# Fused attention and softplus FFN on one core: the reciprocals' store on another queue, another order in the last round, and transposes nobody reads

## The chip, the cores and the metric

One core of one Trainium2 chip. The metric is the device time of one execution in microseconds (us), median of several runs. The engines are TensorE (PE; its weight loads are listed as PEld), VectorE (DVE), ScalarE (ACT), GpSimd (POOL) and SyncE (SP), which here only issues DMAs. TensorE's clock has two levels, 2.4 and 1.2 GHz; the profile prints the granted share, 1.00 and 0.50.

## The reference, cut to what matters

```python
# q, k, v: (4, 8, 576, 64) float32; w_in: (512, 2048), w_out: (2048, 512), given as float64
scores = scale * np.matmul(q, k.transpose(0, 1, 3, 2)) + bias      # bias: a small MLP of log distances
attn = np.exp(scores - np.max(scores, axis=-1, keepdims=True))
attn = attn / (np.sum(attn, axis=-1, keepdims=True) + 1e-09)
x = np.matmul(attn, v).transpose(0, 2, 1, 3).reshape(2304, 512)
h = x @ w_in
out = (np.maximum(h, 0.0) + np.log1p(np.exp(-np.abs(h)))) @ w_out
```

## The kernel before

The work has three stages. The first (to about 65 us) writes the bias table to DRAM (`e_d`). The second is the attention: 16 units n = 0 to 15, each a pair of heads of one batch item. The third is the FFN over blocks of tokens (512 at a time, one of 256), 16 slices of the hidden dimension each, in float32 split in two float32r parts.

One unit of attention has nine score tiles t. `u_s` (L314) computes a tile on TensorE into PSUM (L338; tokens S, Z), adds the bias and takes the minimum on VectorE (L356; A, ZA), and takes the exponential and its row sums on ScalarE (L374; X, ZX). `u_t` (L409) transposes blocks of the exponentials on TensorE (`turn`, L402; T) and copies them from PSUM to `pt` (L310 on ScalarE, L312 on VectorE; V). The letter behind the slash of a T names the PSUM tile that it writes (0 and 1: the two `s` tiles, 2: `t`, o: the tile of the attention output `o`, beside its accumulators); behind a V it names the engine of the copy (a: ScalarE, d: VectorE). `u_pv` (L442) multiplies by v into `o` (L461; P0 to P4; P3 and P4 belong to the unit of the round before). The reciprocals of the row sums (`inv`, L494; I) are transposed (`u_r`, R), copied to a tile `r` of 9 x 128 on ScalarE (L515; C), stored to `r_d` in DRAM (L516), and 24 tokens later read back from there, spread over 64 partitions, as `rb` by three DMAs (L522). `u_x` (L472; O, one round later) multiplies `o` by `rb` on VectorE (L481) into `x`, which four DMAs store to `x_d` (L487 to L490), the input of the FFN. `queue(n)` (L502) picks the queue of the store and of the reads: ScalarE's for units 0 and 1, SyncE's for the others.

The order on every engine is written out by hand: one string of tokens for each round (`ROUND0`, L52, for unit 0, `ROUND` for units 2 to 13, `ROUND15`, L73, for the last), read from left to right by `emit` (L569). The instructions of a token go to the end of their engines' queues in that order, and each engine works through its own in order. Between them stand the loads of later units on SyncE's queue (L98), and the preparation of FFN weights: float64 weights are read (L660), reduced to float32 (L635 to L652; B) and stored (`w_d`, L673).

Round 15 also starts the FFN. Its f tokens name entries of `FIRST` (L82): f2 is `w_fin` (L714) for the first slice of `w_in`, an ScalarE copy (L719) that waits for the load of `w_d` (L691) and a GpSimd subtraction (L721); f3, f0, f7, f9 prepare the four parts of the first block's `x` (L737 on ScalarE, L738 on VectorE), f4 loads the last of them; f11 and f12 are the first two steps, whose matmuls (`emit_h`, L742, L748) write one of four PSUM tiles `h`. PSUM tiles of the attention's scores are given up before round 15, and the `h` tiles lie there.

`es_m` keeps the order as emitted; waits between engines are inserted by the framework where tiles are shared.

Of the kernel before, what the change touches and what calls it, by code (L numbers as in the profile page):

```python
# [9 lines left out]
F32 = mybir.dt.float32  # L10
# [10 lines left out]
B, H, S, D = 4, 8, 576, 64  # L21
# [7 lines left out]
SH = S // 2  # L29
# [20 lines left out]
"""  # L50

ROUND0 = """  # L52
A6 A2 Z7 T10/1 A7 Z3 T20/0 V20/a T30/o A0 T00/2 ZA7 V00/d V30/a V10/a A1 A5 Z8 X7 X2 ZX7 ZA3 X5
X6 ZA8 A3 ZX3 ZX8 Z4 ZA4 ZL1 ZL3 ZX4 A8 T22/2 T40/1 T32/o ZL4 V32/d T02/0 V22/a V02/a T01/o X0
T11/2 V40/d T21/1 V11/a ZL2 V01/d V21/d L2 T12/0 P0 X8 L0 X1 I V12/d T41/1 A4 P1 X4 T31/0 R/2
V41/a C P2 V31/d L3 X3 L4 L1
"""
# [13 lines left out]
"""  # L71

ROUND15 = """  # L73
P3 I T00/2 P4 V00/a T02/2 V02/d f2 T32/2 V32/a T10/2 O R/o V10/a C T01/o V01/a T11/o T12/2 V11/a
V12/a T22/o V22/a f4 P0 T21/2 f3 V21/a f0 P1 T20/2 V20/a f7 T30/2 V30/a T40/2 f8 f1 V40/a f9 f11
B0 T41/2 P2 B1 f5 f10 V41/d f6 T31/2 B2 B3 f12 V31/a B4
"""
ROUND16 = """
P3 P4 O
# [41 lines left out]
def tile_log_bias_attention__then__softplus_ffn(  # L121
# [13 lines left out]
    nc = tc.nc  # L135
# [5 lines left out]
    r_d = dram.tile([16, 9, 128], F32, name="r_d")  # L141
# [9 lines left out]
    ident = const.tile([128, 128], F32, name="ident")  # L151
# [108 lines left out]
    N = 16  # L260
# [120 lines left out]
    def tail(n, i):  # L381

        assert all(("e", n, t) in done for t in TAILS[i])
        done.add(("l", n, i))
        tl = pp.tile([128, 2, 64], F32, tag="tl", name="tl", bufs=9)
        if i < 4:
            src = pairs.pop((n, i))[:, :, 512:S]
        else:
            src = prob[n, 4][:, 512:S].rearrange("p (o c) -> p o c", o=1)
            src = src.to_broadcast([128, 2, 64])  # L390
        nc.gpsimd.tensor_copy(tl, src)
        tails[n, i] = tl.rearrange("p a c -> p (a c)")

    s_use, s_held = [0], set()

    def turn(blocks, on=None):
        ps = ps_o if on == "o" else s_buf[int(on)]
        ps = ps[:, :, SH:SH + 64 * len(blocks)].rearrange("p a (i c) -> p a i c", c=64)
        for i, src in enumerate(blocks):
            for a in range(2):  # L400
                rows = slice(64 * a, 64 * a + 64)
                nc.tensor.transpose(  # L402
                    ps[:, a, i], src[rows], ident[rows, 64 * a:64 * a + 64], tile_position=(64 * a, 0)
                )
        return ps
# [88 lines left out]
    def inv(n):  # L494

        assert all(("e", n, t) in done for t in range(9))
        done.add(("i", n))
        s_ = ssum[n][:, 0:9]
        nc.vector.tensor_scalar(s_, s_, 1e-9, None, op0=ALU.add)
        nc.vector.reciprocal(s_, s_)  # L500

    def queue(n):  # L502
        return nc.scalar if n < 2 else nc.sync

    def u_r(n):

        st_ = {}

        def pe(on=None):
            assert ("i", n) in done  # L510
            st_["ps"] = turn([ssum[n]], on)

        def first():
            r = st.tile([9, 128], F32, tag="r", name="r")
            nc.scalar.activation(r.rearrange("p (a c) -> p a c", a=2), st_["ps"][0:9, :, 0], AF.Copy)  # L515
            queue(n).dma_start(out=r_d[n], in_=r)  # L516

        def second():
            t = op_.tile([128, S], F32, tag="rb", name="rb")
            flat = r_d[n].rearrange("a b -> (a b)").rearrange("(o c) -> o c", o=1)  # L520
            for hd, lo, hi, c0 in ((0, 0, S, 0), (1, 256, S, S), (1, 0, 256, S + 320)):
                queue(n).dma_start(  # L522
                    out=t[64 * hd:64 * hd + 64, lo:hi],
                    in_=flat[:, c0:c0 + hi - lo].to_broadcast([64, hi - lo]),
                )
            rb[n] = t

        return pe, first, second
# [40 lines left out]
    def emit(n, tok):  # L569

        tok, _, on = tok.partition("/")
        on = (on,) if on else ()
        kind, late_ = tok.rstrip("0123456789"), tok[len(tok.rstrip("0123456789")):]
        a = [int(c) for c in late_]

        def stage(key, make, i, *arg):
            if key not in units:
                units[key] = make(*key[1:])
            units[key][i](*arg)

        if kind in ("S", "A", "X"):
            if n + 1 < N:
                stage(("s", n + 1, *a), u_s, "SAX".index(kind))
        elif kind in ("Z", "ZA", "ZX"):
            stage(("s", n, *a), u_s, ("Z", "ZA", "ZX").index(kind))
        elif kind == "L":
            if n + 1 < N:
                tail(n + 1, *a)
        elif kind == "ZL":
            tail(n, *a)  # L590
        elif kind in ("T", "V"):
            stage(("t", n, *a), u_t, "TV".index(kind), *on)
        elif kind == "P":
            stage(("p", n - (a[0] >= PV_LATE), *a), u_pv, 0)
        elif kind == "I":
            inv(n)
        elif kind in ("R", "C"):
            stage(("r", n), u_r, "RC".index(kind), *on)
        elif kind == "O":
            if n:  # L600
                stage(("x", n - 1), u_x, 0)
                defer(8, lambda: stage(("x", n - 1), u_x, 1))
        elif kind == "B":
            if 1 <= n <= len(pre):
                stage(("b", n - 1), u_bits, *a)
                if a[0] == 4:
                    defer(8, lambda: stage(("b", n - 1), u_bits, 5))
        elif kind == "f":
            w, *arg = FIRST[int(late_)]
            FFN[w](*arg)  # L610
        else:
            assert False, tok
# [3 lines left out]
    def defer(k, f):  # L616
        waiting.append([k, f])
# [59 lines left out]
    fp = {}  # L677
# [63 lines left out]
    hs, gs, ys = {}, {}, {}  # L741
    def emit_h(bi, f):  # L742
        nb = blocks[bi][1]
        ps = fp["h"].tile([128, 512], F32, tag="h", name="h")
        i = 0
        for c in range(4):
            for a, x_ in ((0, 0), (0, 1), (1, 0)):
                nc.tensor.matmul(  # L748
                    ps[:, :nb],
                    lhsT=wi[f][:, a, 128 * c:128 * c + 128],  # L750
                    rhs=xs[bi, c][:, x_, :nb],
                    start=(i == 0),
                    stop=(i == 11),
                )
                i += 1
        hs[bi, f] = ps
# [105 lines left out]
    ps_t, ps_o = (ps_a.tile([128, 2, 512], F32, name=nm) for nm in ("t", "o"))  # L862
# [21 lines left out]
    def step(i):  # L884

        new = old = None
        if i < len(seq):
            bi, f = seq[i]
            emit_h(bi, f)
# [156 lines left out]
```

## Time and profile before

| | |
|---|---|
| median of 3 runs | 703.2 us (702.04, 703.2, 712.35) |
| the profiled execution: its own time | 707.46 us |
| its span, first to last instruction | 705.6 us |
| busy share of the span: PE, PEld, DVE, ACT, POOL | 94%, 67%, 71%, 73%, 6% |
| mean granted clock of TensorE | 0.971 |

Times in the rows are microseconds from the start of the span unless marked ns. A row of the timeline gives start, duration, engine, line, operation, out<-in, how many instructions were merged, and in brackets the idle time ahead of them with what ended it. Rows whose engine ends in q (SPq, ACTq) are instructions of a queue that issue DMAs; their duration is the issue, not the transfer. A PE that counts as busy need not run at its peak.

### The profile page before, as it was taken

How to read it: one execution, taken by the hardware profiler on the slowest of the kernel's cores; microseconds unless marked ns; L12 is line 12 of the kernel's file. 1: busy time of each engine (PE TensorE's matmuls, PEld its weight loads, DVE VectorE, ACT ScalarE, POOL GpSimd, SP SyncE). 2: the span in 40 equal slices, each digit the busy share in tenths (PEclk: the TensorE clock that was granted, in tenths of full speed). 3: DMA queues.
4: the chain of work that ended last, by engine and by line, in shares of the span. 5: the costliest groups of instructions: out<-in, count | busy, mean ns of one | idle time of the engine just before them, and what ended most of it. 6: DMA issues, size and time to landing. Idle time of an engine off the chain costs nothing.

```text
span 705.6 us, 13216 instructions
## 1 busy us (share of the span) xinstructions
PE 661.3 (94%) x4800; PEld 475.7 (67%) x4800; DVE 499.8 (71%) x1078; ACT 514.8 (73%) x1062; POOL 40.6 (6%) x106
## 2 busy tenths in 40 slices
PE   5697889998998999599999999999999999999997
PEld 2123446555655665368788888888888888888886
DVE  6996568976887889267888694778686554655564
ACT  6899568986887899477777675886676575665654
POOL 0000111121111111110000000000000000000000
PEclk9898799999999999799999999999999999999999
DMA  5885967677776653545132210521020320402220
GB/s 152 309 275 173 344 177 226 195 227 237 231 232 232 214 182 101 177 124 178 61 135 74 90 59 2 179 90 60 31 90 1 105 75 2 151 28 83 67 84 37
DMA packets 51041, 96.85 MB, mean 137 GB/s; under 512 B 7440, under 2 KB 19104, under 8 KB 50976
## 3 DMA queue, kind: packets, MB, share of 16 engines
q1 hardware_dynamic: 50460, 95.41, 41.3%
q8 instruction: 38, 0.62, 0.4%
q10 hardware_dynamic: 516, 0.60, 0.4%
q14 instruction: 27, 0.22, 0.1%
HBM read 67.98 MB, written 28.01 MB: 136 GB/s over the span
## 4 chain that ended last, share of the span: by engine, by line
PE 77%; DMA 11%; ACT 4%; DVE 3%; SPq 2%; issue 2%; ACTq 0%; DVEq 0%
PE h L748 27%; PE y L806 26%; PE o L461 8%; PE s L338 6%; PE acc L230 3%; PE s L402 3%; DMA r_d<-r 3%; DMA rb<-r_d 2%; DMA e_d<-e 2%; PE t L338 2%; PE t L402 2%; ACT e L251 1%; DMA b<-e_d 1%; PE o L402 1%; SPq L522 1%
## 5 line engine op out<-in xcount | busy, mean ns | idle before, releaser
L748 PE MATMUL h<-x,wi 128*128 128x512 f32 (+1 forms) x960 | 213.9, 372 | 0.1
L806 PE MATMUL y<-wo,g 128*128 128x512 f32 x864 | 209.9, 391 | 0.0
L748 PEld LDWEIGHTS h<-x,wi 128*128 128x128 f32 x960 | 170.4, 190 | 33.9 <-DVE wi L721 0.9
L806 PEld LDWEIGHTS y<-wo,g 128*128 128x128 f32 x864 | 161.3, 188 | 33.7 <-DVE g L780 0.2
L771 DVE SCALAR_TENSOR_TENSOR u<-u,e 128x512 f32<-128x512 f32 (+1 forms) x80 | 51.0, 637 | 102.2 <-ACT l L768 101.9
L374 ACT ACTIVATE p<-p,m 128x576 f32<-128x576 f32 x144 | 110.1, 767 | 8.8 <-DVE m L356 6.7
L764 ACT ACTIVATE e<-h 128x512 f32<-128x512 f32 (+1 forms) x80 | 44.2, 553 | 78.9 <-PE h L748 78.9
L461 PE MATMUL o<-pt,vn 128*64 128x256 f32 (+3 forms) x640 | 91.3, 430 | 0.6 <-ACT pt L310 0.6
L356 DVE CUSTOM_DVE_ANT_0 p<-s,b 128x576 f32<-128x576 f32 x92 | 68.5, 755 | 26.1 <-PE s L338 9.0
L338 PE MATMUL s<-kn,qn 64*128 64x288 f32 (+1 forms) x468 | 69.5, 436 | 0.2 <-ACT p L349 0.2
L778 ACT ACTIVATE g<-l 128x512 fp32r<-128x512 f32 (+1 forms) x80 | 46.8, 585 | 20.4 <-DVE l L775 10.7
L461 PEld LDWEIGHTS o<-pt,vn 128*64 128x64 f32 (+1 forms) x640 | 37.1, 140 | 28.5 <-issue 13.3
L780 DVE TENSOR_TENSOR g<-l,g 128x512 fp32r<-128x512 f32 (+1 forms) x80 | 50.4, 630 | 3.7 <-ACT g L778 3.7
L230 PE MATMUL acc<-m,coef 128*32 128x512 f32 (+17 forms) x352 | 37.7, 527 | 14.5 <-DVE m L217 7.2
L775 DVE TENSOR_TENSOR l<-l,u 128x512 f32<-128x512 f32 (+1 forms) x80 | 50.6, 633 | 0.0
L773 DVE SCALAR_TENSOR_TENSOR l<-h,l 128x512 f32<-128x512 f32 (+1 forms) x80 | 50.5, 631 | 0.0
L768 ACT ACTIVATE l<-u 128x512 f32<-128x512 f32 (+1 forms) x80 | 47.1, 589 | 2.9 <-DVE g L780 0.2
L765 ACT ACTIVATE e<-e 128x512 f32<-128x512 f32 (+1 forms) x80 | 47.2, 590 | 2.5
L767 ACT ACTIVATE u<-e 128x512 f32<-128x512 f32 (+1 forms) x80 | 47.2, 590 | 2.6
L402 PEld LDWEIGHTS s<-ident,p 64*128 64x128 f32 x546 | 26.8, 141 | 29.6 <-issue 8.2
L217 DVE TENSOR_SCALAR m<-lw,pb 128x576 f32<-128x576 f32 (+17 forms) x122 | 44.3, 445 | 0.4 <-PE acc L230 0.4
L338 PEld LDWEIGHTS s<-kn,qn 64*128 64x128 f32 (+1 forms) x468 | 31.0, 176 | 15.4 <-issue 8.4
(66 smaller groups left out, 685.3 us busy)
## 6 DMA issues: line engine op xcount, KB each, us to landing
e_d<-e SPq DMA_DIRECT2D x36, 295.5 KB, 4.0
qn<-in_q_dram SPq DMA_DIRECT2D x16, 576.0 KB, 5.4
b<-e_d SPq DMA_DIRECT2D x32, 288.0 KB, 4.0
r<-in_moe_w_in_dram SPq DMA_DIRECT2D x16, 512.0 KB, 5.1
r<-in_moe_w_out_dram SPq DMA_DIRECT2D x16, 512.0 KB, 3.1
xr<-x_d SPq DMA_DIRECT2D x28, 256.0 KB, 3.4
vn<-in_v_dram SPq DMA_DIRECT2D x16, 320.0 KB, 3.3
kn<-in_k_dram SPq DMA_DIRECT2D x16, 288.0 KB, 6.6
```

The costliest lines, as they stand in the source:

```text
L230: nc.tensor.matmul(acc[32 * g:32 * g + 32, lo:hi], lhsT=coef.rearrange("p o h -> p (o h)"), rhs=hid[s, g][:, lo:hi], start=True, stop=True ...
L338: nc.tensor.matmul(ps[at:at + w, half, :SH], lhsT=q_n[n][rows, hd, c0:c0 + w], rhs=k_n[n][rows, hd], start=True, stop=True, tile_position= ...
L356: nc.vector.tensor_tensor_reduce(prob[n, t].rearrange("p (a c) -> p a c", a=2), st_["ps"], bias[pr, t].rearrange("p (a c) -> p a c", a=2), ...
L374: nc.scalar.activation(p, p, AF.Exp, bias=st_["m"], scale=-1.0, accum_out=ssum[n][:, PLACE.index(t):PLACE.index(t) + 1],)
L402: nc.tensor.transpose(ps[:, a, i], src[rows], ident[rows, 64 * a:64 * a + 64], tile_position=(64 * a, 0))
L461: nc.tensor.matmul(o[up, half, 0:w], lhsT=v_n[n][rows, jb, hd], rhs=pt[n, jb][rows, c0:c0 + w], start=(jb == 0), stop=(jb == 4), tile_posi ...
L748: nc.tensor.matmul(ps[:, :nb], lhsT=wi[f][:, a, 128 * c:128 * c + 128], rhs=xs[bi, c][:, x_, :nb], start=(i == 0), stop=(i == 11),)
L771: nc.vector.scalar_tensor_tensor(u, u, -1.0, e, op0=ALU.add, op1=ALU.subtract)
L773: nc.vector.scalar_tensor_tensor(l, ps, 0.0, l, op0=ALU.max, op1=ALU.add)
L775: nc.vector.tensor_tensor(l, l, u, op=ALU.subtract)
L780: nc.vector.tensor_tensor(g[:, 1], l, g[:, 0], op=ALU.subtract)
L806: nc.tensor.matmul(y, lhsT=g[:, a, 128 * ts:128 * ts + 128], rhs=wo[f][:, w_], start=(first and i == 0), stop=(last and i == 2),)
```

## The change

Three things. (1) The store of the reciprocals, L516, is issued from ScalarE's queue in every unit; the reads back (L522) stay where they were. (2) A new token D*k* issues k transposes of the 128 x 128 identity by itself on TensorE; nothing reads what they write. In round 0 (D6 ahead of Z8, D14 ahead of T22) they write columns 288 to 415 of the first bank of the tile `o`, cells that only the transposes marked /o use; in round 15 (D4, D4, D6) they write one of the four `h` tiles, which the FFN's first step then takes over. (3) Round 15 gets another order: T32 and its copy go from behind V02 to behind V01, and its copy from ScalarE to VectorE; the copy V02 goes from VectorE to ScalarE, V01, V22 from ScalarE to VectorE, V41 from VectorE to ScalarE; f2 goes from ahead of T32 to behind T12, ahead of V11; I goes behind T00; B0 goes ahead of f11.

```diff
@@ -50,8 +50,8 @@
 """
 
 ROUND0 = """
-A6 A2 Z7 T10/1 A7 Z3 T20/0 V20/a T30/o A0 T00/2 ZA7 V00/d V30/a V10/a A1 A5 Z8 X7 X2 ZX7 ZA3 X5
-X6 ZA8 A3 ZX3 ZX8 Z4 ZA4 ZL1 ZL3 ZX4 A8 T22/2 T40/1 T32/o ZL4 V32/d T02/0 V22/a V02/a T01/o X0
+A6 A2 Z7 T10/1 A7 Z3 T20/0 V20/a T30/o A0 T00/2 ZA7 V00/d V30/a V10/a A1 A5 D6 Z8 X7 X2 ZX7 ZA3 X5
+X6 ZA8 A3 ZX3 ZX8 Z4 ZA4 ZL1 ZL3 ZX4 A8 D14 T22/2 T40/1 T32/o ZL4 V32/d T02/0 V22/a V02/a T01/o X0
 T11/2 V40/d T21/1 V11/a ZL2 V01/d V21/d L2 T12/0 P0 X8 L0 X1 I V12/d T41/1 A4 P1 X4 T31/0 R/2
 V41/a C P2 V31/d L3 X3 L4 L1
 """
@@ -71,9 +71,9 @@
 """
 
 ROUND15 = """
-P3 I T00/2 P4 V00/a T02/2 V02/d f2 T32/2 V32/a T10/2 O R/o V10/a C T01/o V01/a T11/o T12/2 V11/a
-V12/a T22/o V22/a f4 P0 T21/2 f3 V21/a f0 P1 T20/2 V20/a f7 T30/2 V30/a T40/2 f8 f1 V40/a f9 f11
-B0 T41/2 P2 B1 f5 f10 V41/d f6 T31/2 B2 B3 f12 V31/a B4
+P3 T00/2 D4 I P4 V00/a T02/2 D4 V02/a T10/2 D6 O R/o V10/a C T01/o V01/d T32/2 V32/d T11/o T12/2 f2 V11/a
+V12/a T22/o V22/d f4 P0 T21/2 f3 V21/a f0 P1 T20/2 V20/a f7 T30/2 V30/a T40/2 f8 f1 V40/a f9 B0
+f11 T41/2 P2 B1 f5 f10 V41/a f6 T31/2 B2 B3 f12 V31/a B4
 """
 ROUND16 = """
 P3 P4 O
@@ -392,6 +392,7 @@
         tails[n, i] = tl.rearrange("p a c -> p (a c)")
 
     s_use, s_held = [0], set()
+    spare = {}
 
     def turn(blocks, on=None):
         ps = ps_o if on == "o" else s_buf[int(on)]
@@ -513,7 +514,7 @@
         def first():
             r = st.tile([9, 128], F32, tag="r", name="r")
             nc.scalar.activation(r.rearrange("p (a c) -> p a c", a=2), st_["ps"][0:9, :, 0], AF.Copy)
-            queue(n).dma_start(out=r_d[n], in_=r)
+            nc.scalar.dma_start(out=r_d[n], in_=r)
 
         def second():
             t = op_.tile([128, S], F32, tag="rb", name="rb")
@@ -605,6 +606,12 @@
                 stage(("b", n - 1), u_bits, *a)
                 if a[0] == 4:
                     defer(8, lambda: stage(("b", n - 1), u_bits, 5))
+        elif kind == "D":
+            if n == N - 1 and "h" not in spare:
+                spare["h"] = fp["h"].tile([128, 512], F32, tag="h", name="h")
+            to = spare["h"][:, 0:128] if n == N - 1 else ps_o[:, 0, SH:SH + 128]
+            for _ in range(a[0]):
+                nc.tensor.transpose(to, ident, ident)
         elif kind == "f":
             w, *arg = FIRST[int(late_)]
             FFN[w](*arg)
@@ -741,7 +748,9 @@
     hs, gs, ys = {}, {}, {}
     def emit_h(bi, f):
         nb = blocks[bi][1]
-        ps = fp["h"].tile([128, 512], F32, tag="h", name="h")
+        ps = spare.pop("h", None)
+        if ps is None:
+            ps = fp["h"].tile([128, 512], F32, tag="h", name="h")
         i = 0
         for c in range(4):
             for a, x_ in ((0, 0), (0, 1), (1, 0)):
```

## Rows read from the trace of the kernel before

**Rows 1.** What TensorE waited for, 60 to 310 us: total us, times, longest

```profile
PE o L402 <- DVE x L481: 11.5, 7, 3.7
```

**Rows 2.** The FFN: us, busy us by engine, clock, DMA share, GB/s

```profile
340.00:705.00 365.00, 361.98 (x1678) 301.91 (x1676) 241.95 (x429) 246.04 (x437) 0.00 (x0) 1.00 0.21 71
```

**Rows 3.** Three rounds, cut at the first L481 of each (columns as rows 2)

```profile
144.96:161.59 16.63, 13.29 (x164) 8.16 (x164) 11.57 (x30) 12.20 (x30) 2.33 (x6) 1.00 0.74 232
...
161.59:176.16 14.57, 13.69 (x144) 8.40 (x144) 11.48 (x29) 10.83 (x27) 2.33 (x6) 0.88 0.72 238
...
258.47:271.55 13.08, 13.08 (x170) 8.09 (x166) 11.60 (x31) 11.71 (x29) 2.33 (x6) 1.00 0.38 120
```

**Rows 4.** Timeline of TensorE: the transposes behind L481 of units 5 and 9

```profile
162.47 0.40 PE L402 MATMUL o<-ident,p 64*128 64x64 f32 x6 [3.34 <-DVE x L481]
...
219.62 0.41 PE L402 MATMUL o<-ident,p 64*128 64x64 f32 x6 [2.13 <-DVE x L481]
```

**Rows 5.** Timeline of SyncE: stores of units 5 and 9, reads of unit 5

```profile
152.39 0.30 SPq L516 DMA_DIRECT2D r_d<-r  x1
...
156.24 1.73 SPq L522 DMA_DIRECT2D rb<-r_d  x3
...
210.80 0.30 SPq L516 DMA_DIRECT2D r_d<-r  x1
```

**Rows 6.** Timeline of ScalarE: copies of units 5 and 9, store of unit 0

```profile
149.56 0.25 ACT L515 ACTIVATE r<-s 9x128 f32<-9x128 f32 x1
...
207.91 0.25 ACT L515 ACTIVATE r<-s 9x128 f32<-9x128 f32 x1
...
79.94 0.55 ACTq L516 DMA_DIRECT2D r_d<-r  x1
```

**Rows 7.** DMA issues: queue, count, KB each, median us to landing

```profile
rb<-r_d ACTq DMA_DIRECT2D x2, 144.0 KB, 5.5
...
rb<-r_d SPq DMA_DIRECT2D x14, 144.0 KB, 2.8
```

**Rows 8.** Timeline of TensorE in round 15: T02, T32, T10, P0, step 0

```profile
283.31 0.40 PE L402 MATMUL t<-ident,p 64*128 64x64 f32 x6
...
284.43 0.40 PE L402 MATMUL t<-ident,p 64*128 64x64 f32 x6 [0.72 <-DVE pt L312]
...
288.11 0.58 PE L402 MATMUL t<-ident,p 64*128 64x64 f32 x6 [3.28 <-ACT pt L310]
...
292.98 2.19 PE L461 MATMUL o<-pt,vn 128*64 128x256 f32 x8 [0.58 <-ACT pt L310]
...
299.65 4.61 PE L748 MATMUL h<-x,wi 128*128 128x512 f32 x12
```

**Rows 9.** Timeline of ScalarE in round 15: the copy of f2

```profile
287.05 0.63 ACT L719 ACTIVATE wi<-a 128x512 fp32r<-128x512 f32 x1 [3.79 <-DMA a<-w_d]
```

**Rows 10.** Timeline of TensorE in round 0: Z8, T22, P0, and P2 later

```profile
65.60 1.33 PE L338 MATMUL t<-kn,qn 64*128 64x288 f32 x4 [1.48 <-DVE pt L312]
...
70.38 0.59 PE L402 MATMUL t<-ident,p 64*128 64x64 f32 x6 [2.28 <-ACT p L374]
...
75.07 2.19 PE L461 MATMUL o<-pt,vn 128*64 128x256 f32 x8
...
79.53 1.19 PE L461 MATMUL o<-pt,vn 128*64 128x256 f32 x8
```

**Rows 11.** Transposes L402 into t, whole span: ns min/median/max

```profile
L402 PEld LDWEIGHTS t<-ident,p x408: 134/138/227, 63.7 to 305.8; 64*128 64x128 f32 x136
...
L402 PE MATMUL t<-ident,p x408: 216/222/367, 63.8 to 305.8; 64*128 64x64 f32 x136
```

**Rows 12.** Two stretches in round 15, all instructions (columns as rows 2)

```profile
297.00:300.00 3.00, 1.74 (x22) 1.06 (x19) 1.15 (x2) 2.23 (x5) 0.16 (x1) 1.00 0.82 265
...
300.00:303.00 3.00, 3.00 (x9) 2.37 (x8) 0.99 (x1) 1.75 (x4) 2.82 (x3) 0.54 0.28 53
```

**Rows 13.** The first of them, L402 alone: us, PE, PEld, clock, DMA

```profile
297.00:300.00 3.00, 1.14 (x16) 0.76 (x16) 1.00 0.82 265
```

## The prediction

> **What bounds the kernel now.** I read the waits of TensorE first, then the rounds, then the queues behind the longest waits. From 340 us on TensorE is busy for 362.0 of 365 us at full clock [rows 2]: the FFN runs at its own pace, and what is gained before it is kept only if the FFN starts sooner. The change touches only the stretch before. There TensorE loses time mostly at one place: the transposes into `o` wait for the multiplication L481, 11.5 us in seven waits [rows 1]. One of the seven, the longest with 3.7 us, belongs to unit 0, whose store already goes by ScalarE's queue; 7.8 us are left for units 2 to 10. A round without such a wait takes 13.08 us, all of it busy on TensorE [rows 3]. The reader is to see there that the round of the longest remaining wait took 16.63 us, and that the next one still took 14.57 us, with a mean clock of 0.88: a long wait is paid twice, once as idle time and once at the lower clock.
>
> **The store, part by part.** L481 waits for `rb`, `rb` for the landing of the store, and the store for its place in SyncE's queue. For unit 5 the copy to `r` ends at 149.56 + 0.25 = 149.81 us [rows 6] and the store is issued at 152.39 [rows 5], behind loads: 2.58 us late. For unit 9 the copy ends at 208.16 and the store is issued at 210.80: 2.64 us late. On ScalarE's queue it stands right behind the copy (unit 0's at 79.94 us is the row for it [rows 6]). The first read of `rb` for unit 5 follows 3.85 us behind its store [rows 5], so the landing bounds it. If the landing takes as long from the other queue, the read moves by 2.58 us. Some of that may be lost, since the same loads are then still under way; I take 2.2. That leaves 3.34 - 2.2 = 1.1 us of unit 5's wait [rows 4]. The 2.13 us of unit 9 [rows 4], which is no longer than that and after which no lower clock is paid, speaks for the clock staying up: 14.57 - 13.08 = 1.49 us more. Unit 5 gives 3.7, unit 9 its 2.1. The four others hold 11.5 - 3.7 - 3.34 - 2.13 = 2.3 us together; where the store was hardly late there is nothing to move, so I take 0.7 of it. Sum 6.5 us. Bounds: 2, if the reads only wait for the loads that the store waited for; 7.8 + 1.5 = 9.3, if every wait goes.
>
> The Trainium skill (Trainium Kernel Development and Optimization, Key Constraints) says that DMAs of all issuing queues share the same engines, and that spreading them only saves issue time. By that the gain would be the lateness alone, 2.58 and 2.64 us at the two stores, and nothing for a store that was not late. The trace agrees as far as it goes: the 144 KB reads landed 5.5 us after issue from ScalarE's queue and 2.8 from SyncE's [rows 7], so that queue is no shortcut.
>
> **Its price on ScalarE.** The issue takes 0.55 us [rows 6], and behind it stand the rest of the weights' preparation, the exponentials and the copies of `pt`. Fourteen stores are added, 14 x 0.55 = 7.7 us of ScalarE. In the round of 13.08 us it is busy for 11.71 [rows 3], so 1.37 us of idle time hides 0.55. I take 0. If the cover were gone, TensorE would wait at the copies of `pt` for up to 7.7 us in all.
>
> **Round 15.** Before, T10 waits 3.28 us for the copy V32 [rows 8], because V32 stands behind f2's copy on ScalarE, which waits 3.79 us for its weights and starts at 287.05 [rows 9]. Behind the change: T02 at about 283.6 (four transposes ahead of it), V02 0.5, T10 at 284.6, six transposes to 285.6, R, the copy to `r` at 286.1, T01 at 286.2, V01 on VectorE to 287.0, T11 at 287.1 with V32 beside it, T12 at 287.6. On ScalarE f2's copy runs from 287.05 as before, V11 and V12 follow to about 288.7, T22 stands at 288.3, its copy ends at 289.2 and P0 starts at 289.5. It stood at 292.98 [rows 8]: 3.5 us. What is late next is f2 again, now ahead of V11, but with little waiting behind it. From P0 to step 0 (6.67 us) tokens and copies are nearly the same, so step 0 moves by the same 3.5 us and the FFN with it. Bounds: 0.3, if V11 inherits the wait of V32; 6.7, if the clock also stays up there. The moves of I, B0 and of the copies V22, V41 cost nothing: VectorE and ScalarE both have gaps there.
>
> **The transposes.** No row shows a 128 x 128 one. The nearest are the half-sized ones, 222 ns median and 367 at most, their weight loads 138 and 227 [rows 11]; six of them take 0.40 us in the fast clock and 0.58 in the slow one [rows 8], so they overlap. I take 0.1 to 0.24 us for one of the new ones: D6 0.6 to 1.4, D14 1.4 to 3.4. In round 0 they lie in waits of 1.48 and 2.28 us [rows 10]. D6 must first wait for the copy that reads the cells it writes, so up to 0.6 us stick out; up to 1.1 of D14. What stands behind both is ScalarE's and VectorE's work, so I cost them at 0. In round 15 their time is in the sum above.
>
> Do they hold the clock? Before the fall to 0.54 behind 300 us, TensorE was busy for 1.74 of 3 us at full clock [rows 12], and 1.14 of these were transposes [rows 13]: here a stretch mostly of transposes went ahead of a fall. That is one case, and I take it that the new ones don't hold it, a gain of 0 in round 0. Bounds: if they do, P0 takes 1.19 instead of 2.19 us [rows 10], P1 and the small ones give as much again, 2.0 us; if they stick out, -1.7.
>
> The Trainium skill (TensorE: Matmul & The Clock Gate, Part 4: PE-mode transpose) says that transpose mode does not engage the full clock, as it does not count as busy time in the same way. By that rule the new transposes give nothing but their cost and the sum is the forecast's, 693.2 us; if they did hold the clock it would be the first rival's, 688.0. The trace agrees with the rule as far as its one stretch goes, 1.14 us of transposes ahead of a fall [rows 13].
>
> **The sum.** 6.5 + 3.5 = 10.0 us off the profiled execution's 707.46 us (span 705.6 and 1.9 around it): 697.5 us. That execution is 4.26 us above the median of 703.2; with the same distance, 693.2 us.
>
> **The rivals.**
> *The clock is held in both rounds.* Then 2.0 us more in round 0, and in round 15 the 1.0 of P0, 0.6 of P1 and some 1.6 of step 0's first 4.61 us [rows 8] (at the full clock it could lose up to half): 693.2 - 5.2 = 688.0. For it speaks that the gaps are filled nearly end to end; against it, rows 12 and 13.
> *The store gains nothing by its queue.* The reads then still wait for the loads on the way; 2 instead of 6.5: 697.7. For it: DMA busy for 0.74 of that round [rows 3], and rows 7. Against it: the loads were issued before, and the store was late by 2.6 us in just the two rounds with long waits.
> *f2's wait moves to V11.* 0.3 instead of 3.5: 696.4. For it: the weights land at 287 us, whatever the order. Against it: by then T10, R, T01, T11 are done.
> *The transposes don't overlap: slower.* Each loads its weights and runs alone at the slow clock, 0.227 + 0.367 = 0.59 us, 34 x 0.59 = 20.1 us. Waits of 1.48 + 2.28 in round 0 [rows 10] and 0.72 in round 15 [rows 8] hide 4.5; 15.6 stick out in TensorE's own chain: 708.8. It decides from (10.0 + 4.5) / 34 = 0.43 us for one transpose. For it: they are all on one tile of cells and fill the whole array, where the half-sized ones come in pairs. Against it: the FFN's full-array matmuls overlap their loads, 302 us of loads beside 362 us of matmuls [rows 2].
>
> **How the numbers follow.** Forecast 0.56 (own range 689 to 697.5), clock held 0.17, store without gain 0.13, f2's wait moved 0.07, slower 0.04, others 0.03. The range reaches from a held clock with a little more, 686.5, to the store without gain with a little less, 699.5. A change of over 2%, about what a measurement of this kernel can tell, means below 689.1 or above 717.3 us. Below: most of the held clock (0.13) and the lower end of the forecast (0.07), 0.20. Above: 0.03, if the last rival comes with more. Within: 0.77.
>
> **What would show it.** Right: stores within 0.1 us of the copy to `r` in all units; waits for L481 of units 5 and 9 at 1.1 us or less; rounds 5 to 10 within 0.5 us of 13.1; P0 of round 15 some 10 us earlier than before; the FFN with the same busy share. Wrong: waits for L481 that sum to over 9 us, TensorE waiting for copies of `pt` in the middle rounds, transposes of over 0.4 us, or TensorE's granted clock at 0.5 (1.2 GHz) for longer than before.

## The result and the profile after

The median went from 704.47 us (4 runs, 702.04 to 712.35) to 696.9 us (4 runs, 694.49 to 705.41). The ratio is 0.9886, 95% interval 0.9847 to 0.9924: 8.0 us less (5.4 to 10.8), where 10.0 were forecast. It is less than 2%. The ratios here and below leave out executions over 1.5% above the kernel's fastest: 705.41 us here, and one each of e4 (710.79), e7 (706.44) and e10 (1073.39, at a mean clock of 0.558). The profiled execution took 696.38 us. In what follows, the lines L482, L517, L523, L614 are those of the changed kernel: the multiplication by `rb`, the store, the reads, and the new transposes; other lines behind L394 are one to nine higher than in the kernel before.

The page of the changed kernel: TensorE's busy share went from 94% to 95%, and the mean granted clock from 0.971 to 0.985.

```profile
span 694.5 us, 13234 instructions
...
PE 659.5 (95%) x4821; PEld 475.2 (68%) x4821; DVE 501.8 (72%) x1079; ACT 514.2 (74%) x1061; POOL 40.8 (6%) x106
```

What TensorE waited for from 60 to 310 us in the changed kernel (total us, times, longest). The 11.5 us at the transposes behind the multiplication [rows 1] are 2.3. New in the middle rounds are waits of P for ScalarE's copies of `pt`, 1.23 us at unit 5 and 0.55 at unit 9 (L462 <- L310). The 3.1 us are T22's in round 0, the last row is of round 15.

```profile
PE t L403 <- ACT p L374: 3.1, 1, 3.1
PE o L403 <- DVE x L482: 2.3, 2, 1.6
PE o L462 <- ACT pt L310: 1.8, 2, 1.2
...
PE o L403 <- ACT pt L310: 1.2, 1, 1.2
```

What ScalarE waited for from 90 to 285 us in the changed kernel. It shows where waits have come up instead: the two groups ahead of the copy L642, the first instruction behind the store, come to 6.6 us, and the trace of before has no wait of ScalarE for a DMA there.

```profile
ACT a L642 <- DMA b<-e_d: 4.9, 2, 2.8
...
ACT a L642 <- DMA x_d<-x: 1.7, 2, 1.3
```

Stretches of the changed kernel, cut at the first L482 of units 4, 5, 6 and of 8, 9, 10, then an undisturbed round, the FFN, and the two ends of the attention (us; busy us of PE, PEld, DVE, ACT, POOL; clock; DMA share; GB/s).

```profile
138.81:155.51 16.70, 15.03 (x166) 8.39 (x163) 11.65 (x32) 11.70 (x29) 2.27 (x6) 0.90 0.78 240
155.51:169.71 14.20, 14.20 (x190) 9.05 (x192) 11.73 (x33) 12.19 (x30) 2.27 (x6) 1.00 0.70 215
...
195.91:210.37 14.46, 13.47 (x166) 7.95 (x164) 11.54 (x29) 11.64 (x29) 2.27 (x6) 1.00 0.83 266
210.37:224.47 14.10, 13.68 (x172) 8.35 (x170) 11.72 (x32) 11.94 (x32) 2.28 (x6) 1.00 0.77 255
250.52:263.60 13.08, 13.08 (x170) 8.08 (x166) 11.63 (x31) 11.70 (x29) 2.26 (x6) 1.00 0.33 108
...
340.00:694.00 354.00, 350.89 (x1630) 292.76 (x1628) 232.13 (x412) 238.11 (x423) 0.00 (x0) 1.00 0.21 72
...
60.00:104.00 44.00, 35.58 (x417) 21.42 (x415) 28.45 (x79) 32.51 (x81) 5.82 (x16) 0.92 0.75 253
...
275.00:305.00 30.00, 25.64 (x182) 15.95 (x181) 15.98 (x27) 19.19 (x39) 5.22 (x7) 0.89 0.49 152
```

The last two stretches of the kernel before, for comparison:

```profile
60.00:104.00 44.00, 33.34 (x354) 18.24 (x348) 25.41 (x70) 29.19 (x73) 4.96 (x16) 0.81 0.74 238
...
275.00:305.00 30.00, 22.56 (x194) 13.62 (x192) 12.34 (x27) 17.87 (x43) 6.97 (x10) 0.77 0.48 147
```

The reader is to see two things. The round with unit 5's wait is as long as before, 16.70 us against 16.63 [rows 3], although TensorE hardly waits for L482 in it. And the clock, which the forecast left alone, went from 0.81 to 0.92 at the beginning of the attention and from 0.77 to 0.89 at its end.

**Unit 5, where the forecast saw most.** ScalarE in the changed kernel, around the store of unit 5:

```profile
143.49 0.25 ACT L516 ACTIVATE r<-s 9x128 f32<-9x128 f32 x1
146.18 0.27 ACTq L517 DMA_DIRECT2D r_d<-r  x1
146.55 0.68 ACT L642 ACTIVATE a<-r 128x512 f32<-128x512 f32 x1 [2.81 <-DMA b<-e_d]
...
280.68 0.63 ACT L726 ACTIVATE wi<-a 128x512 fp32r<-128x512 f32 x1 [2.16 <-DMA a<-w_d]
```

The copy ends at 143.74 us, and the store is issued at 146.18: 2.44 us late, where it had been 2.58 us late on SyncE. Unit 9's is 1.72 us late (before 2.64), unit 10's 0.95; all others follow their copies by 0.03 us. The bracket of L642 names the DMA that landed last ahead of it; what ScalarE stood at is the wait in front of its own store, as the semaphores of the trace show below. (The last row is of round 15, for later.) SyncE's queue in the same stretch says why:

```profile
139.69 1.52 SPq L489 DMA_DIRECT2D x_d<-x  x1
141.26 0.59 SPq L490 DMA_DIRECT2D x_d<-x  x1
141.90 0.60 SPq L491 DMA_DIRECT2D x_d<-x  x1
142.54 0.58 SPq L300 DMA_DIRECT2D b<-e_d  x1
143.59 0.46 SPq L304 DMA_DIRECT2D b<-e_d  x1
144.83 0.46 SPq L305 DMA_DIRECT2D b<-e_d  x1
145.55 0.38 SPq L302 DMA_DIRECT2D b<-e_d  x1
146.03 0.38 SPq L667 DMA_DIRECT2D r<-in_moe_w_out_dram  x1
```

In this trace every DMA counts up one of eight semaphores on landing. They are taken in turn, in program order, by the DMAs of SyncE's and ScalarE's queues alike. Ahead of a DMA its queue waits until the DMA eight before, on the same semaphore, has landed. The eight rows begin with the `x_d` store at 139.69 and end just ahead of the store of unit 5, so these two share one: the `x_d` store landed at 146.10, ScalarE's wait for that semaphore ended at 146.12, and the store was issued at 146.18. For unit 9 the same count leads to the `x_d` store issued at 197.10. In the kernel before, the same two stores stood behind the same two DMAs, which landed at 151.84 and 209.84 us: 2.04 of unit 5's 2.58 us and 1.68 of unit 9's 2.64 were this wait, and only the rest was SyncE's queue. So on either of the two queues the store waits for its place, and here it takes ScalarE with it. TensorE then waits for the copies of `pt` that stand behind it on ScalarE, and the clock falls. In the rows of TensorE, those below 80 us are of round 0 and those above 270 of round 15; they are read further down.

```profile
63.93 0.87 PE L614 MATMUL o<-ident 128*128 128x128 f32 x6 [0.60 <-ACT pt L310]
...
66.15 0.33 PE L614 MATMUL o<-ident 128*128 128x128 f32 x1
...
69.60 0.58 PE L403 MATMUL t<-ident,p 64*128 64x64 f32 x6 [3.12 <-ACT p L374]
...
72.84 2.19 PE L462 MATMUL o<-pt,vn 128*64 128x256 f32 x8
...
149.16 0.76 PE L462 MATMUL o<-pt,vn 128*64 128x320 f32 x4 [1.23 <-ACT pt L310]
...
151.45 2.13 PE L462 MATMUL o<-pt,vn 128*64 128x256 f32 x8
...
277.13 0.87 PE L614 MATMUL h<-ident 128*128 128x128 f32 x6
...
281.74 0.58 PE L403 MATMUL o<-ident,p 64*128 64x64 f32 x6 [1.18 <-ACT pt L310]
283.05 2.19 PE L462 MATMUL o<-pt,vn 128*64 128x256 f32 x8 [0.72 <-DVE pt L312]
...
290.24 3.02 PE L757 MATMUL h<-x,wi 128*128 128x512 f32 x12
```

From the end of the copy to the multiplication unit 5 took 155.51 - 143.74 = 11.77 us; before it was 161.59 - 149.81 = 11.78. The sum is the same, its parts are not. The last read of `rb` landed 11.67 us behind the copy before (161.47) and 10.38 now (154.12). But the multiplication had to stand behind another operation on VectorE, which waited for TensorE:

```profile
154.81 0.76 DVE L356 CUSTOM_DVE_ANT_0 p<-s,b 128x576 f32<-128x576 f32 x1 [1.64 <-PE s L338]
```

So `rb` came 1.3 us sooner, and TensorE, held up by ScalarE's copies and then at the low clock, came late itself: the wait for L482 vanished from the list without any time being won. A row of the wait list that shrinks is not yet a gain.

**Where the 11.1 us between the two profiled spans went.** Cut at the first multiplication of units 0, 1 and 13 and at step 0 of the FFN, the stretches were 90.82, 13.08, 167.65, 28.10 and 405.91 us; they are 87.48, 11.94, 164.19, 26.64 and 404.25. That is 3.3 + 1.1 us up to the multiplications of units 0 and 1 (0.8 of the 3.3 was there ahead of the first new transpose: the same transposes at the beginning of round 0 stand at 61.84 us, before at 62.63), 3.5 in the middle rounds, 1.5 in round 15, and 1.7 behind it, nearly all in step 0, whose matmuls took 4.61 us [rows 8] and now take 3.02. In the middle, the rounds cut by units 5, 6, 9 and 10 gave only 0.9 us together, and those of units 4 and 8, whose stores had not been late by more than 0.3 us, gave 1.2 and 0.8.

### The profile page after: what moved, and what is told of

It is laid out like the page before. It is cut to its first block, busy times and chain, and to the rows that moved or that the text cites. A ratio compares the mean times of both kernels' runs of the same rounds, so it can differ in the third digit from the quotient of the medians.

```text
span 694.5 us, 13234 instructions
## 1 busy us (share of the span) xinstructions
PE 659.5 (95%) x4821; PEld 475.2 (68%) x4821; DVE 501.8 (72%) x1079; ACT 514.2 (74%) x1061; POOL 40.8 (6%) x106
## 4 chain that ended last, share of the span: by engine, by line
PE 76%; DMA 10%; ACT 6%; DVE 3%; issue 2%; SPq 2%; ACTq 1%; DVEq 0%
PE y L815 28%; PE h L757 28%; PE o L462 6%; PE s L338 5%; PE acc L230 3%; DMA b<-e_d 3%; ACT p L374 2%; PE s L403 2%; PE t L338 2%; DMA qn<-in_q_dram 2%; DMA e_d<-e 1%; DMA r_d<-r 1%; PE t L403 1%; ACT e L251 1%; DMA rb<-r_d 1%
## 5 line engine op out<-in xcount | busy, mean ns | idle before, releaser
L462 PE MATMUL o<-pt,vn 128*64 128x256 f32 (+3 forms) x640 | 92.6, 433 | 2.5 <-ACT pt L310 1.8
L787 ACT ACTIVATE g<-l 128x512 fp32r<-128x512 f32 (+1 forms) x80 | 46.8, 585 | 20.3 <-DVE l L784 10.7
L462 PEld LDWEIGHTS o<-pt,vn 128*64 128x64 f32 (+1 forms) x640 | 37.0, 141 | 31.2 <-issue 14.1
```

What stands on the lines that cost most here:

```text
L462: nc.tensor.matmul(o[up, half, 0:w], lhsT=v_n[n][rows, jb, hd], rhs=pt[n, jb][rows, c0:c0 + w], start=(jb == 0), stop=(jb == 4), tile_posi ...
```

## The experiments

The chips were not the same for all experiments; each kernel is compared with runs of the kernel before on its own chip. At 707 us, 0.01 of a ratio is 7 us. The clock is the mean granted clock, in the third column over the executions that the ratio uses, and of the profiled one in two stretches. One thing about the change holds for all of them: `emit` reads a token's digits one by one (`a = [int(c) for c in late_]`, and D takes `a[0]`), so D14 issues one transpose and not fourteen, and D10 one and not ten. The row at 66.15 us above is all of D14. The changed kernel has 6 + 1 + 4 + 4 + 6 = 21 new transposes, not 34.

| kernel | ratio, 95% interval | mean clock | 60 to 104 us | 275 to 305 us |
|---|---|---|---|---|
| before | 1 | 0.973 | 0.81 | 0.77 |
| e1, store alone | 0.9980 (0.9954, 1.0007) | 0.977 | 0.81 | 0.77 |
| e2, order alone | 0.9979 (0.9950, 1.0009) | 0.974 | 0.81 | 0.83 |
| e3, transposes of round 0 alone | 0.9993 (0.9965, 1.0021) | 0.976 | 0.84 | 0.77 |
| e4, all but transposes | 0.9939 (0.9910, 0.9967) | 0.978 | 0.81 | 0.72 |
| e5, changed kernel | 0.9891 (0.9849, 0.9934) | 0.985 | 0.88 | 0.77 |
| e6, without those of round 0 | 0.9891 (0.9842, 0.9941) | 0.981 | 0.84 | 0.89 |
| e7, matmuls for transposes | 0.9871 (0.9825, 0.9917) | 0.986 | | |
| e8, loads moved | 0.9863 (0.9820, 0.9906) | 0.982 | 0.92 | 0.89 |
| e9, store on GpSimd | 0.9901 (0.9865, 0.9938) | 0.984 | 0.88 | 0.94 |
| e10, second store | 0.9912 (0.9880, 0.9944) | 0.985 | 0.84 | 0.77 |
| e11, more transposes | 0.9887 (0.9849, 0.9926) | 0.985 | 0.88 | 1.00 |
| e12, e8 and e11 | 0.9837 (0.9789, 0.9884) | 0.986 | 0.92 | 1.00 |

**e1: the kernel before with the store on ScalarE, and nothing else.**

```diff
-            queue(n).dma_start(out=r_d[n], in_=r)
+            nc.scalar.dma_start(out=r_d[n], in_=r)
```

> Only part 1 of the change: the store of the reciprocals on ScalarE's queue in all units. By the prediction's step (the lateness on SyncE is gone) it gains 6.5 us against the kernel before, and ScalarE does not wait at the store. By the rival that the trace of after suggests (the store still has to wait for an earlier DMA at units 5, 9 and 10, now on ScalarE, and the copies of pt behind it come late) it gains about 3.5 us, with waits of 1 to 2.5 us on ScalarE behind L515 in those units.

Measured: 0.2% less, and no difference is inside the interval (3.3 us less to 0.5 more). The stores of units 5, 9 and 10 were 3.00, 1.18 and 1.60 us behind their copies. The waits of TensorE in this kernel: those for the multiplication fell to 4.3 us. Of the 8.3 us for ScalarE's copies, 3.9 are T10's in round 15, which this run leaves as it was, and 2.2 stand ahead of P at units 5 and 10.

```profile
PE t L402 <- ACT pt L310: 5.5, 4, 3.9
PE o L402 <- DVE x L481: 4.3, 5, 2.0
PE o L461 <- ACT pt L310: 2.8, 3, 1.8
```

And those of ScalarE, 7.3 us ahead of the copy behind the store (L635 here):

```profile
ACT a L635 <- DMA x_d<-x: 3.9, 3, 2.0
ACT a L635 <- DMA b<-e_d: 3.4, 1, 3.4
```

The wait changes its place without the transposes and without the new order too: it is the store's own.

**e2: the kernel before with the new order of round 15, no transposes.**

```diff
-P3 I T00/2 P4 V00/a T02/2 V02/d f2 T32/2 V32/a T10/2 O R/o V10/a C T01/o V01/a T11/o T12/2 V11/a
+P3 T00/2 I P4 V00/a T02/2 V02/a T10/2 O R/o V10/a C T01/o V01/d T32/2 V32/d T11/o T12/2 f2 V11/a
...
```

> Only the new order of round 15, without the new transposes and with the store as before. By the prediction: 3.5 us less. By the rival that f2's wait only moves to V11: 0.3 us less. If the step from L481 of unit 14 to the first step's matmuls is read from the trace: 15.36 us before, near 12 by the first, near 15 by the second.

Measured: 1.5 us less, from 3.5 less to 0.6 more. In its profile step 0 starts 12.81 us behind the first multiplication of round 15, before 299.65 - 284.29 = 15.36: 2.55 us, of the 3.5 forecast. The other profiles lie the same way: 15.83 and 15.90 with the old order (e1, e3), 14.06 with the new one and no transposes (e4), 12.31 to 14.31 with them (changed kernel, e5, e6, e8 to e10). In the whole time the gain is at the limit of what these runs can tell.

**e3: the kernel before with the transposes of round 0.**

```diff
-A6 A2 Z7 T10/1 A7 Z3 T20/0 V20/a T30/o A0 T00/2 ZA7 V00/d V30/a V10/a A1 A5 Z8 X7 X2 ZX7 ZA3 X5
-X6 ZA8 A3 ZX3 ZX8 Z4 ZA4 ZL1 ZL3 ZX4 A8 T22/2 T40/1 T32/o ZL4 V32/d T02/0 V22/a V02/a T01/o X0
+A6 A2 Z7 T10/1 A7 Z3 T20/0 V20/a T30/o A0 T00/2 ZA7 V00/d V30/a V10/a A1 A5 D6 Z8 X7 X2 ZX7 ZA3 X5
+X6 ZA8 A3 ZX3 ZX8 Z4 ZA4 ZL1 ZL3 ZX4 A8 D14 T22/2 T40/1 T32/o ZL4 V32/d T02/0 V22/a V02/a T01/o X0
...
```

> Only the transposes of round 0 (6 and 14), all else as before. By the prediction (they don't hold the clock): no difference, within 1 us. By the rival (they hold it): 2 to 4.5 us less, L481 of unit 1 at about 99.5 us instead of 103.9, and the time at the lower clock between 60 and 100 us under 8 us instead of 17.

Measured: 0.5 us less, from 2.5 less to 1.5 more. The clock in the first stretch is 0.84, against 0.81 before. The fall, at 64.7 us before, came at 71.0 us. So these transposes, seven as issued, put the fall off but don't keep the clock up, and alone they are worth nothing that can be measured.

**e4: the changed kernel with no transposes.**

```diff
-A6 A2 Z7 T10/1 A7 Z3 T20/0 V20/a T30/o A0 T00/2 ZA7 V00/d V30/a V10/a A1 A5 D6 Z8 X7 X2 ZX7 ZA3 X5
-X6 ZA8 A3 ZX3 ZX8 Z4 ZA4 ZL1 ZL3 ZX4 A8 D14 T22/2 T40/1 T32/o ZL4 V32/d T02/0 V22/a V02/a T01/o X0
+A6 A2 Z7 T10/1 A7 Z3 T20/0 V20/a T30/o A0 T00/2 ZA7 V00/d V30/a V10/a A1 A5 D0 Z8 X7 X2 ZX7 ZA3 X5
+X6 ZA8 A3 ZX3 ZX8 Z4 ZA4 ZL1 ZL3 ZX4 A8 D0 T22/2 T40/1 T32/o ZL4 V32/d T02/0 V22/a V02/a T01/o X0
...
-P3 T00/2 D4 I P4 V00/a T02/2 D4 V02/a T10/2 D6 O R/o V10/a C T01/o V01/d T32/2 V32/d T11/o T12/2 f2 V11/a
+P3 T00/2 D0 I P4 V00/a T02/2 D0 V02/a T10/2 D0 O R/o V10/a C T01/o V01/d T32/2 V32/d T11/o T12/2 f2 V11/a
```

> The changed kernel with all its new transposes left out (token counts kept). They feed nothing, so the output is the same. By the prediction: the time of the changed kernel within 1 us. By the rival (they hold the clock in round 0): 2 to 4.5 us more than the changed kernel, with 14 to 17 us at the lower clock between 60 and 100 us.

Measured: 4.3 us less (2.3 to 6.4). Store and order together give this; their single values, 1.4 and 1.5, add up to 2.9, within the intervals. The forecast's two terms were 10.0 together.

**e5: the changed kernel once more, beside e6 to e8 on one chip.** The kernel is unchanged, so there is no diff.

> The changed kernel once more, for more runs beside those of its parts. Nothing but scatter is expected: 0.984 to 0.993 of the kernel before.

Measured: 7.7 us less (4.7 to 10.7), as in the first result. The stores of units 5, 9 and 10 are late by 2.49, 1.18 and 1.12 us, the same three units. In its round 15 the clock is 0.77, as before, where the first profile had 0.89: what the transposes do there is not the same in every execution.

**e6: without the transposes of round 0.**

The edit is that of e4, in round 0's two lines only:

```diff
-X6 ZA8 A3 ZX3 ZX8 Z4 ZA4 ZL1 ZL3 ZX4 A8 D14 T22/2 T40/1 T32/o ZL4 V32/d T02/0 V22/a V02/a T01/o X0
+X6 ZA8 A3 ZX3 ZX8 Z4 ZA4 ZL1 ZL3 ZX4 A8 D0 T22/2 T40/1 T32/o ZL4 V32/d T02/0 V22/a V02/a T01/o X0
...
```

> The changed kernel without the 20 new transposes of round 0 (token counts kept); they feed nothing. If the transposes of round 15 make the difference between the changed kernel and the one without any (about 0.5%), this one stands with the changed kernel, and its clock is down for at most 7 us between 275 and 305 us. If those of round 0 make it, it stands with the kernel without any. By the prediction both kinds give nothing and all three are the same within 1 us.

Measured: the same ratio as e5, 0.9891. So the seven transposes of round 0 can't be seen in the time. The clock in round 0 is 0.84, and was 0.88 in e5.

**e7: true matmuls of the identity in place of the transposes (D3, D7, D2, D2 and D3).**

```diff
-                nc.tensor.transpose(to, ident, ident)
+                nc.tensor.matmul(to, lhsT=ident, rhs=ident, start=True, stop=True)
...
```

> The changed kernel with true matmuls of the identity in place of the new transposes, half as many (3, 7, 2, 2, 3), into the same cells that nothing reads. If a transpose counts for less than a matmul with the clock, this holds it more often: 1 to 3 us less than the changed kernel, and less time at the lower clock in rounds 0 and 15. If both count alike: no difference within 1 us. If a float32 matmul of that size takes far more than 0.25 us, the matmuls stick out of the waits and it is slower.

Measured: 0.9871, not to be told from e5. It differs from e5 in more than the kind of the work, since ahead of T22 it has seven matmuls where e5 has one transpose. Its profile, of the 706.44 us, isn't compared. Whether matmuls hold the clock better than transposes stays open.

**e8: four loads of later units moved in the order, so that others stand eight before the stores.**

```diff
-LOADS = {22: "b", 4: "q", 0: "v", 34: "w", 6: "k", 25: "b", 23: "b", 10: "b", 31: "b"}
+LOADS = {66: "b", 4: "q", 0: "v", 34: "w", 6: "k", 70: "b", 68: "b", 10: "b", 72: "b"}
```

> The changed kernel with the loads of the bias tiles that stand ahead of C (tokens 22, 23, 25, 31) moved behind the reads of rb (66, 68, 70, 72). If the store waits on ScalarE for its turn behind an earlier DMA that these loads hold up, the waits of 1.7 to 2.4 us behind L515 in units 5 and 9 fall under 0.5 us and the middle rounds lose 3 us or more. If the store waits for something else, the waits stay. If the loads now hold up the reads of the next round's data, TensorE shows new waits for the bias or for q and k.

Measured: 0.9863. The stores of units 5 and 9 now follow their copies by 0.03 us, and those of units 4, 6 and 10 are late by 0.72, 1.68 and 2.84. Their wait ended in each case with the landing of the load of `qn` that stands eight before. ScalarE around the stores of units 5 and 10 in this kernel:

```profile
145.06 0.25 ACT L516 ACTIVATE r<-s 9x128 f32<-9x128 f32 x1
145.34 0.27 ACTq L517 DMA_DIRECT2D r_d<-r  x1
145.66 0.69 ACT L642 ACTIVATE a<-r 128x512 f32<-128x512 f32 x1 [0.35 <-ACT r L516]
...
215.41 0.27 ACTq L517 DMA_DIRECT2D r_d<-r  x1
215.73 0.68 ACT L642 ACTIVATE a<-r 128x512 f32<-128x512 f32 x1 [3.16 <-DMA x_d<-x]
```

Nothing about the store was changed, nor its queue; the loads ahead of it are others, and so is the DMA eight before it. That moved the wait to other units. By itself the run leaves it open whether the moved traffic did this, but the semaphores settle it: in the nine profiles with the store on ScalarE (e7 left out), 30 stores are over 0.2 us late, and each was issued 0.08 us behind a landing on its own semaphore. The expected 3 us in the middle rounds did not come: from unit 1's multiplication to unit 13's it took 166.35 us, and 162.87 in e5 on the same chip. What units 5 and 9 gained was paid elsewhere.

**e9: the store on GpSimd's queue for units 2 to 15.**

```diff
-            nc.scalar.dma_start(out=r_d[n], in_=r)
+            (nc.scalar if n < 2 else nc.gpsimd).dma_start(out=r_d[n], in_=r)
```

> The changed kernel with the store issued from GpSimd's queue for units 2 to 15. If what was left of the gain in the middle rounds is eaten by ScalarE standing still at the store (1.7 to 3 us at units 5, 9 and 10) and by the late copies of pt behind it, ScalarE's waits at L642 for an earlier DMA go, TensorE's waits for copies of pt in the middle go, and it is 1 to 3 us faster. If the store's lateness is what counts, whoever waits, the waits come back at L481 (2 to 3 us at units 5 and 9) and the time stays. If GpSimd's way of issuing takes 1 us or more longer to land, L481 waits more and it is slower by 1 to 4 us.

Measured: 0.9901. The store is issued 0.29 to 0.30 us behind the copy in all fourteen units, never late, and ScalarE has no wait for a DMA at L642. Yet TensorE's waits for the multiplication are back:

```profile
PE o L403 <- DVE x L482: 9.9, 8, 2.5
```

From the copy to the multiplication unit 5 takes 9.41 us and unit 9 takes 9.96, where the least of any unit of the middle rounds is 8.11 us. So a store that is never late still leaves 1.3 to 1.8 us. In unit 5 the first read was issued 3.37 us behind the store, just behind its landing, and the last read landed 5.5 us later: landing and reads are slow by themselves in these rounds, with DMA busy for 0.78 and 0.83 of the time in the changed kernel's. Another queue for the store doesn't take that away; in e8, with other loads ahead, the two units take 8.12 and 8.11 us. GpSimd's stores count up eight semaphores of their own, so they stand outside the turn.

**e10: a second store of the same tile, read by nobody, behind the first on ScalarE.**

```diff
+    r2_d = dram.tile([16, 9, 128], F32, name="r2_d")
...
             nc.scalar.dma_start(out=r_d[n], in_=r)
+            nc.scalar.dma_start(out=r2_d[n], in_=r)
```

> The changed kernel with every store of the reciprocals issued twice on ScalarE's queue, the second time into DRAM rows that nothing reads. By the prediction's step (ScalarE has room) the second issue of 0.27 us is hidden: the time of the changed kernel within 1 us. By the rival that every DMA on ScalarE's queue has to wait its turn behind an earlier DMA, the second store adds waits of its own at L642 in the rounds with bias loads, 1 to 4 us more.

Measured: 0.9912, some 1.5 us above the changed kernel and inside its interval. The waits of ScalarE for DMAs ahead of the copy behind the stores are 8.1 us, where they were 6.6; L644 is that copy here, and the row not shown has 0.9:

```profile
ACT a L644 <- DMA b<-e_d: 7.2, 4, 3.0
```

The second issue, 0.27 us, is not quite hidden: the rounds without a late store, those of units 11 to 13, took 13.24 to 13.26 us, where they took 12.97 to 13.08 in the changed kernel. The first store shows no such price: 13.08 us of such a round before [rows 3] and in the changed kernel. So most of what the first store costs ScalarE is its turn.

**e11: more transposes in round 15, in the waits ahead of P0.** D10 and D6 were meant as sixteen; D10 issues one, so it is seven more.

```diff
-P3 T00/2 D4 I P4 V00/a T02/2 D4 V02/a T10/2 D6 O R/o V10/a C T01/o V01/d T32/2 V32/d T11/o T12/2 f2 V11/a
-V12/a T22/o V22/d f4 P0 T21/2 f3 V21/a f0 P1 T20/2 V20/a f7 T30/2 V30/a T40/2 f8 f1 V40/a f9 B0
+P3 T00/2 D4 I P4 V00/a T02/2 D4 V02/a T10/2 D6 O R/o V10/a C T01/o V01/d T32/2 V32/d T11/o T12/2 D10 f2 V11/a
+V12/a T22/o D6 V22/d f4 P0 T21/2 f3 V21/a f0 P1 T20/2 V20/a f7 T30/2 V30/a T40/2 f8 f1 V40/a f9 B0
```

> The changed kernel with 16 more transposes of the identity in round 15, 10 behind T12 and 6 behind T22, where TensorE waits for 1.2 and 0.7 us ahead of P0. At 0.107 us each they take 1.7 us and fit the waits. If such transposes help to hold the clock, it is not down between P0 and the first step more often than not, P0 takes 1.19 instead of 2.19 us, and 1 to 3 us go. If they count for nothing with the clock, P0 stays at 2.2 us and the time is the changed kernel's within 1 us.

Measured: 0.9887, no less than the changed kernel. But the clock did not fall in round 15 at all, and P0 and P1 ran at the full clock. TensorE in this kernel, D10, D6, P0 and step 0:

```profile
287.31 0.33 PE L614 MATMUL h<-ident 128*128 128x128 f32 x1
...
288.20 0.87 PE L614 MATMUL h<-ident 128*128 128x128 f32 x6
289.00 1.19 PE L462 MATMUL o<-pt,vn 128*64 128x256 f32 x8
...
290.45 1.19 PE L462 MATMUL o<-pt,vn 128*64 128x256 f32 x8
...
293.90 3.04 PE L757 MATMUL h<-x,wi 128*128 128x512 f32 x12
```

P0 took 2.19 us in the changed kernel and takes 1.19; from P0 to step 0 it is 4.90 us, against 290.24 - 283.05 = 7.19. The stretch in which the gain is expected has it; but unit 1's multiplication stood at 106.68 us in this execution, against 99.41, and 4.1 of that was there at D6 of round 0 (68.02 us, against 63.93), a stretch in which both kernels have the same instructions. Over six executions the scatter of such differences covers the gain.

**e12: e8 and e11 together.**

> The changed kernel with both edits at once: sixteen more transposes in round 15 (ten ahead of f2, six ahead of the copy V22), and four of the loads of later units moved in the order (tokens 22, 23, 25, 31 to 66, 68, 70, 72). Theory (the transposes keep the clock up; the store's delay is the turn of the DMAs' completions, not a queue): the low-clock stretch of round 15 is 3.4 us or less, step 0 of the FFN starts 11 to 12 us behind the first L482 of round 15's unit (15.4 before), the stores of units 5 and 9 follow their copies at once, and another store, of units 4 to 10, waits 0.5 to 3 us in their place; 694 to 698 us, ratio 0.982 to 0.988. Rival (the transposes' help in round 15 was one execution's luck): a low-clock stretch of 6.8 us or more there, step 0 some 12.5 to 14.5 us behind, ratio 0.986 to 0.991.

Measured: 698.12 us beside 707.82, ratio 0.9837, 11.5 us less (8.2 to 14.9): the lowest ratio of all, 0.979 to 0.988, and lower than the changed kernel by half a per cent, with intervals that overlap. Its last stretch:

```profile
275.00:305.00 30.00, 26.98 (x241) 17.07 (x240) 18.45 (x36) 22.54 (x48) 6.95 (x10) 1.00 0.54 172
```

The clock stayed up in round 15 once more, in the second execution out of two with these transposes. Step 0 starts 11.71 us behind the first multiplication of round 15. The store of unit 5 follows at once, unit 9's is 0.75 us late, and units 6 and 10 pay 2.91 and 3.40 us in their place: the turn moves the wait and does not end it.

## Why the prediction was right, and where it was not

The time, 696.9 us, lies in the forecast's own range of 689 to 697.5, and the gain is 8.0 of 10.0 us. The terms of the sum are another matter.

**The store, 6.5 us: mis-sized, and its reason was wrong.** The step that failed reads: "On ScalarE's queue it stands right behind the copy". It stands 2.44 us behind it in unit 5, because the DMAs' turn goes with it to every queue that shares the eight semaphores. The forecast took the place in SyncE's queue as the cause of the lateness; most of it was the turn. Units 5 and 9 were to give 5.8 us and the rounds that they disturb gave 0.9. The others were to give 0.7 and gave 2.6. Alone, the store measured 1.4 us (0.5 more to 3.3 less, e1), below the lower bound of 2 in the middle. The profiles of the same chip say the same: from unit 1's multiplication to unit 13's they have 167.21 and 167.19 us with the store on SyncE (e2, e3), and 166.51 and 166.02 on ScalarE (e1, e4). The rival "the store gains nothing by its queue" (2 us) was nearer, and e9 shows its mechanism: a punctual store still waits for landings. The Trainium skill's sentence that spreading DMAs over queues only saves issue time (Trainium Kernel Development and Optimization, Key Constraints) agrees with that: 9.9 us of waits were left with no store late.

**ScalarE's price, 0: right for the issue, wrong for the wait.** The issue takes 0.27 us, not the 0.55 of unit 0, and is hidden (rounds of 13.08 us before and after). What was not priced is that an issue can itself have to wait, and holds up the copies behind it: 1.8 us of TensorE's waits at L462, and 2.13 us for a P that takes 1.19 at the full clock. The prediction named this sign, "TensorE waiting for copies of `pt` in the middle rounds", as one that would prove it wrong, and for this term it did.

**Round 15, 3.5 us: right in direction, too large.** T10's wait is gone. P0 moved from 292.98 to 283.05, 9.93 us earlier, where "some 10 us" were forecast; but 8.36 of these came from earlier rounds, and P0 stands only 7.12 us behind the multiplication, before 8.69. The rival "f2's wait moves to V11" is there in part: f2's copy waits 2.16 us for its weights, and the transposes ahead of P0 wait 1.18 us for the copy behind it. From P0 to step 0, where 6.67 us were to stay, it is 7.19. So step 0 stands 14.31 us behind the multiplication, before 15.36: 1.05 us, of 3.5. Alone the order showed 2.55 us in its profile and 1.5 us (0.6 more to 3.5 less) in the time.

**The transposes' cost: right.** Six take 0.87 us, and one alone 0.33, so one more takes (0.87 - 0.33) / 5 = 0.11 us, the low end of 0.1 to 0.24. The slower rival, 0.43 us, is out. But the forecast priced 34 and 21 came: D14 gave one, so the wait ahead of T22 that it was to fill was left open (3.12 us at 69.60, before 2.28 [rows 10]).

**The clock, 0: too low as far as is known, right at the place named.** Without the transposes (e4) the gain is 4.3 us, with them 8.0 and 7.7 (first result and e5); so they seem to be worth some 3.5 us (3.4 and 3.7). This is argued, not shown: the intervals of e4 and e5 overlap a little, they ran on different chips, and of the 6.4 us between their two profiled spans 3.2 lie between the multiplications of units 1 and 13, where both kernels have the same instructions. P0 of round 0 took 2.19 us as before [rows 10], so there "they don't hold it" was right. But the low clock lasted a shorter time: 44 x (1 - 0.81) x 2 = 16.7 us of the first stretch were spent at 1.2 GHz before, and 44 x (1 - 0.92) x 2 = 7.0 after. The mean clock over the executions agrees: on e4's chip it went from 0.973 to 0.978, on e5's from 0.975 to 0.985. This also bears on the Trainium skill's rule (TensorE: Matmul & The Clock Gate, Part 4: PE-mode transpose) that transposes don't engage the full clock. The runs differ from it so far: with seven transposes in the waits, the granted clock stayed at 2.4 GHz longer in round 0, and in both profiled executions with seven more of them (e11, e12) it did not fall in round 15. The measurement decides here, for this kernel; why it does is not shown, since e7 told matmuls and transposes not apart, and the trace prints both as MATMUL.

So the sum came out right by luck, because two errors stood against each other: 10.0 - 4.3 = 5.7 us too much for store and order, and some 3.7 that the sum left out, probably the transposes'. Which of the two rounds' transposes would bring them is shown only weakly: those of round 0 alone gave 0.5 us (e3), and leaving them out of the changed kernel cost nothing (e6).

## What to carry to other kernels

Before a DMA is moved to another queue, find what its issue waits for: if that is the landing of an earlier DMA, the wait goes with it, and on a computing engine everything behind it in order waits too. When a wait vanishes from one engine's list, compare the stretch from the producer to the consumer, here 11.78 against 11.77 us, before calling it a gain. Price a wait of TensorE together with the clock behind it, and try cheap unread work in the waits just ahead of the matmuls that would run at the low clock. Count new instructions in the profile before reading anything into them: fourteen were one here.

## What the runs showed of the hardware

- The completion semaphores, eight in turn over SyncE's and ScalarE's DMAs, tie the issue of one DMA to the landing of another that has nothing to do with it (2.44 us at unit 5). GpSimd's stores, on eight others, did not wait in this way in e9.
- The mean granted clock and the time go together from one execution to the next. Over 69 executions of the kernel before the correlation is -0.63, and 0.01 of clock goes with 4.0 us; over 163, of the kernel before and of e1 to e12, it is -0.86 and 6.2 us. At 700 us, 0.01 of the mean clock is 14 us at half speed, so each of these goes with 0.3 to 0.4 us. Which of the two moves the other, a correlation doesn't show.
- Seven unread transposes of 128 x 128 put the fall of the clock in round 0 off, at 0.11 us each: it came between 64.7 and 67.4 us in the profiles of before, e1, e2, e4 and e6, which have none there, and between 68.4 and 74.1 in those of the changed kernel, e3, e5 and e8 to e12, which have them. Counted from the same transposes at the beginning of the round (61.84 us in the changed kernel), which takes out the scatter of the stage before, it is 2.1 to 4.6 us without and 6.4 to 8.4 with them.
